# A linear-attention and two-layer MLP kernel: the first two chunks loaded in 128-row transfers, narrowed in single operations and re-ordered

## The chip, the cores and the metric

One core of a Trainium2 chip runs one program of five engines: TensorE (PE in the rows; its weight loads are PEld), VectorE (DVE), ScalarE (ACT), GpSimd (POOL) and SyncE (SP), which here only issues transfers (DMAs). The metric is the device time of one execution in microseconds, lower is better; the kernel before is given as the median of three runs.

## The reference, cut to what matters

```python
kv  = einsum('bhsd,bhse->bhde', k, v)        # 8 batches, 8 heads, 576 tokens, 64 dims
out = einsum('bhsd,bhde->bhse', q, kv)
x   = out / sqrt(mean(out * out, -1) + 1e-6) * g_norm   # -> 4608 tokens x 512
h   = x @ w_in;   y = maximum(0.01 * h, h) @ w_out      # 512 -> 2048 -> 512
h   = y @ w_in2                                          # again 512 -> 2048 -> 512
out = (P3(h) / (1 + |b0||h| + |b1|h*h + 1e-6)) @ w_out2
```

## The kernel before, in words

The 4608 tokens are worked in nine chunks of 512. All products of the two MLPs are done in three matmuls each: a value is split into a high part of reduced precision (xh, gh, w) and the rest (xl, gl), and low times high, high times high and high times low are added up (`mm3`). So one block of 128 of the 2048 hidden columns costs a chunk 12 matmuls of 128x512 for `ph` (the first product) and 12 for `y` (the second). The weights arrive as 64-bit words, 512 KB for a part (one block's first or second weight), and each part is narrowed to 32 bits on the chip before it can be used: one step on ACT (`narrow_abs`), four on DVE in a chain (`narrow`: clamp L160, shift L161, sign L164, low bits L167), then the split: `hi` on ACT (L361) and the difference `lo` (L132).

The first MLP's weights are narrowed while the first chunks already run. That start is written out by hand: the table `STARTUP` is a list of steps, and each engine gets its instructions in the order of that list, in one queue that is never re-ordered. A step is a name with arguments: `kv,b,i,at` loads tile i of the keys and values of batch b (token rows by 512 k columns and 512 v columns), `q,c,g,at` half g of the queries of chunk c, `w,k,i` weight part i of pair k; `km` adds a kv tile's products into a batch's 64x64 states (on TensorE), `ev` copies these out of PSUM (ACT); `po` multiplies the queries with the states, `sq`, `pm`, `nr`, `nw`, `bc` are the RMS norm (squares on ACT, their means on TensorE, the inverse root on ACT and DVE, its spread over the rows on TensorE), `oc` copies po out with the gain, `xw` scales it on DVE, `xh` and `xl` split it; `h`, `lk`, `gl`, `y` are the first MLP; `ab`, `na`, `hi`, `lo` narrow and split a weight part. `wu,n` issues n matmuls on a constant tile (`warm`), whose results nobody reads. A step with `,g` at its end runs its difference on POOL. Chunk 0 and the first six blocks come first, then chunk 1 with the same six blocks; the loop over `units` takes over after that, and there `prep` does the attention of the next chunk in slots between the blocks.

Transfers: SP issues them in the list's order, and with eight semaphores a ninth transfer is issued only when the one eight before it has landed. A batch has 576 tokens, so its five kv tiles have 128, 128, 128, 128 and 64 rows; a half of the queries comes as two transfers of 64 rows of the chip's memory each (`load_q`), so that the two heads of a pair lie above each other as `mm_out` wants them.

The change touches `STARTUP`, `KT`, `load_gain`, `narrow`, `load_q`, `mm_kv`, `evac_kv`, the `p_` functions of these steps, the slot of one load in `prep` and the last output copy (L724 to L731).

Of the kernel before, what the change touches and what calls it, by code (L numbers as in the profile page):

```python
# [8 lines left out]
F32 = mybir.dt.float32  # L9
F32R = mybir.dt.float32r  # L10
U32 = mybir.dt.uint32
# [11 lines left out]
    q,0,0,w0_8 q,0,1,w0_9 tl c kv,0,4,w0_10 w,0,0 kv,0,3,w0_11 kv,0,1,w0_12 kv,0,2,w1_6 kv,0,0,w1_7 wu,14 w,2,0  # L23
    w,0,1 w,1,0 kv,1,2,w1_8 kv,1,4,w0_7 wu,4 g kv,1,1,w1_9 kv,1,0,w1_5 km,0,4 kv,1,3,w0_6 wu,2 wu,6 km,0,3
    km,0,1 w,2,1 ab,0,0 na,0,0 q,1,1,raw q,1,0,raw hi,0,0 w,1,1 km,0,0 km,0,2 wu,6 ev,0 ab,0,1 po,0,1 na,0,1
    po,0,0 ab,1,0 sq,0,1 w,3,0 km,1,2 w,3,1 sq,0,3 ab,2,0 na,1,0 sq,0,2 hi,0,1 wu,8 lo,0,1,g pm,0,1 sq,0,0
    km,1,4 cg pm,0,0 w,4,0 na,2,0 lo,0,0 km,1,1 oc,0,3,w0_11 hi,1,0 oc,0,1,w0_10 nr,0,w0_8 nw,0 wu,2 lo,1,0,g
    hi,2,0 km,1,3 oc,0,0,w0_10 km,1,0 w,5,0 oc,0,2,w0_11 bc,0,0 ev,1 lo,2,0 bc,0,1 xw,0,0 xw,0,2 ab,2,1 xw,0,1
    xh,0,0 xh,0,1 po,1,1 xw,0,3 xl,0,1,g xh,0,2 xh,0,3 sq,1,3 sq,1,2 po,1,0 pm,1,1 xl,0,0 ab,1,1 sq,1,0 xl,0,3
    xl,0,2,g h,0,0 h,0,2 na,2,1 ab,3,0 oc,1,1,w0_12 ab,3,1 sq,1,1 na,1,1 w,5,1 lk,0,0 hi,2,1 na,3,1 w,4,1 w,6,1  # L30
    lo,2,1,g hi,1,1 hi,3,1 lo,1,1,g oc,1,2,w1_6 pm,1,0 oc,1,0,w0_12 nr,1,w0_9 lo,3,1 h,0,1 ab,4,1 ab,5,0
    oc,1,3,w1_6 gl,0,0 y,0,0 ab,5,1 ab,4,0 na,3,0 lk,0,1 nw,1 na,5,1 lk,0,2 hi,3,0 bc,1,1 h,0,3 gl,0,1 hi,5,1
    xw,1,3 y,0,1 xh,1,3 w,6,0 xw,1,2 lo,3,0,g na,4,1 lo,5,1,g ab,6,1 w,8,1 bc,1,0 h,0,4 lk,0,3 gl,0,2,g hi,4,1
    xh,1,2 ab,6,0 na,5,0 lo,4,1,g hi,5,0 w,8,0 na,4,0 lk,0,4 gl,0,3,g hi,4,0 xw,1,0 gl,0,4 w,7,1 lo,4,0,g
# [8 lines left out]
def kernel(  # L43
# [27 lines left out]
    KT = [(i * P, min(P, S - i * P)) for i in range((S + P - 1) // P)]  # L71
# [46 lines left out]
    def load_gain():  # L118
        for j in range(P // D):
            nc.sync.dma_start(out=gsc[j * D:(j + 1) * D, :], in_=g_norm.rearrange("(p o) -> p o", o=1))  # L120
# [35 lines left out]

    def narrow(ts, u):

        uf = u.bitcast(F32)
        nc.vector.tensor_scalar(out=uf, in0=uf, scalar1=TOP_MIN, scalar2=TOP_MAX, op0=ALU.max, op1=ALU.min)  # L160
        nc.vector.tensor_scalar(out=u, in0=u, scalar1=3, scalar2=0x3FFFFFFF,  # L161
                                op0=ALU.logical_shift_left, op1=ALU.bitwise_and)
        for i, t in enumerate(ts):
            nc.vector.scalar_tensor_tensor(out=u[:, i, :], in0=words(t, U32)[1], scalar=0xC0000000, in1=u[:, i, :],  # L164
                                           op0=ALU.bitwise_and, op1=ALU.bitwise_or)
        for i, t in enumerate(ts):
            nc.vector.scalar_tensor_tensor(out=u[:, i, :], in0=words(t, U32)[0], scalar=29, in1=u[:, i, :],  # L167
                                           op0=ALU.logical_shift_right, op1=ALU.bitwise_or)
# [73 lines left out]
    with tc.manual_schedule():  # L242
        Y = {}
        G = {}
        with ExitStack() as actx:
# [5 lines left out]
            KV = {}  # L251

            def home(at):

                if at == "raw":
                    return raw()
                return wp.tile([P, 2, N], F32, tag=at, name="raw")
# [97 lines left out]

            def w1_hi(k, i=None):
# [29 lines left out]
            nk = len(KT)  # L386
            HALF = 6
# [21 lines left out]
            def p_kv(bt, i, at="raw"):  # L409
                ss["kv", bt, i] = load_kv(bt, i, at)  # L410

            def p_km(bt, i):
                if bt not in acc:
                    acc[bt], made[bt] = bank("att" if bt else "h", "kvacc"), 0
                mm_kv(i, ss.pop(("kv", bt, i)), acc[bt], made[bt] == 0, made[bt] == nk - 1)
                made[bt] += 1

            def p_ev(bt):
                evac_kv(bt, acc.pop(bt))

            def p_q(c, g, at="raw"):
                qs[c, g] = load_q(c, g, at, (nc.sync, nc.sync if c else nc.scalar))

            def p_po(c, g):
                for p in (2 * g, 2 * g + 1):
                    po[c, p] = bank(f"y{p}", "po")
                mm_out(c, g, qs.pop((c, g)), (po[c, 2 * g], po[c, 2 * g + 1]))
# [20 lines left out]
            def p_pm(c, g):  # L448
# [3 lines left out]
                for p in (2 * g, 2 * g + 1):  # L452
                    mm_ms(p, ss.pop((c, p)), pm[c])

            def p_nr(c, at):
                t = home(at)
                rr[c], ww[c] = t[:, 0, :], t[:, 1, :]
                norm_act(pm[c], rr[c], ww[c])

            def p_nw(c):  # L460
                norm_dve(pm[c], rr[c], ww[c])

            def p_bc(c, g):
                for p in (2 * g, 2 * g + 1):
                    bc[c, p] = bank("h" if c == 0 and g == 0 else "att", "bc")
                    r = slice(32 * p, 32 * (p + 1))
                    nc.tensor.matmul(out=bc[c, p], lhsT=spread[r], rhs=ww[c][r], start=True, stop=True)
# [16 lines left out]
            def p_lk(c, f):  # L484
                if (c, f // 2) not in G:
                    G[c, f // 2] = new_g()
                t = tt[c, f] = leaky(hh.pop((c, f)))
                nc.scalar.activation(out=G[c, f // 2][0][:, f % 2, :], in_=t, func=AF.Copy)
# [12 lines left out]
            def p_table():  # L501
# [11 lines left out]
            def prep(c, po_at, ms_at, w_at, x_at, bursts):  # L513
# [46 lines left out]
                def load_w():  # L560

                    t = st["b"] = squares()
                    for j in range(P // D):
                        (nc.sync, nc.scalar)[j].dma_start(out=t[j * D:(j + 1) * D], in_=rs[c].rearrange("(p r) n -> r p n", r=32)[j:j + 1]
                                          .to_broadcast([D, NC, N]))
# [8 lines left out]
                for g in range(NC // 2):  # L574
                    at(po_at[g], "load", ldq, g)
# [136 lines left out]
        def emit_y2():  # L712
# [11 lines left out]
            else:  # L724
                for e in range(NC):
                    t = raw(1)[:, 0, :]
                    if e % 2:
                        nc.vector.tensor_copy(out=t, in_=ys[e])
                    else:
                        nc.scalar.copy(out=t, in_=ys[e])  # L730
                    nc.sync.dma_start(out=out[pc - NCH, e], in_=t)  # L731
# [83 lines left out]
```

## Time and profile before

| | us |
|---|---|
| median of 3 runs (1663.96 to 1664.95) | 1664.94 |
| the profiled execution, its own time | 1663.81 |
| its span, first to last instruction | 1661.9 |
| PE busy in the span | 1646.3 |
| DVE busy | 920.2 |
| ACT busy | 817.3 |
| POOL busy | 193.1 |

The profiled execution takes 1.9 us outside its span. PE is busy for 99% of the span, so its time is mostly a fixed amount of matmul work; the sum of busy times is an average over stages, though, and the stage that the change edits is a few per cent of the span at its start. The trace tells for each instruction when it ran, how long its engine had been idle before it, and which event ended that idle time; for the transfers, what rate a stretch had; and for TensorE the clock that was granted (1.00 is 2.4 GHz, 0.50 is 1.2 GHz).

### The profile page before, as it was taken

The page shows a single profiled execution, that of the slowest core. Times are in us where ns is not written, and L with a number is a line of the kernel's source. Part 1 is how long each engine was busy: PE and PEld are TensorE (multiplying, and loading weights), DVE is VectorE, ACT ScalarE, POOL GpSimd, SP SyncE. Part 2 cuts the span into 40 slices and gives each one's busy share as a digit, 9 for nine tenths or more (in the row PEclk, how much of TensorE's full clock was granted, in tenths as well). Part 3 has the DMA queues.
Part 4 walks back from the last instruction along what each step waited for, and adds up shares of the span by engine and source line. Part 5 has one row for each costly group of instructions (what it writes and reads, how often), then busy time and mean ns, then how long its engine had stood idle before and what let it go on. Part 6 is the DMA issues. An engine that isn't in the chain of part 4 may idle for free.

```text
span 1661.9 us, 19228 instructions
## 1 busy us (share of the span) xinstructions
PE 1646.3 (99%) x7938; PEld 1336.5 (80%) x7938; DVE 920.2 (55%) x1045; ACT 817.3 (49%) x1080; POOL 193.1 (12%) x91
## 2 busy tenths in 40 slices
PE   8999999999999999999999999999999999999999
PEld 5688778878787887878888888888888888888887
DVE  5858133333342323322337767777767677777776
ACT  4545333333433233332437566655666656666555
POOL 1300000000000000000001222122222222221221
PEclk9999999999999999999999999999999999999999
DMA  9334635152432433220421010101010100001000
GB/s 295 98 126 153 179 107 152 56 166 70 151 103 102 114 89 108 68 79 0 153 89 51 1 51 1 51 1 51 1 51 1 50 2 23 29 1 51 1 26 26
DMA packets 43175, 121.56 MB, mean 73 GB/s; under 512 B 4817, under 2 KB 4817, under 8 KB 43089
## 3 DMA queue, kind: packets, MB, share of 16 engines
q1 hardware_dynamic: 40896, 116.15, 22.1%
q10 hardware_dynamic: 2192, 4.19, 1.1%
q8 instruction: 62, 1.02, 0.3%
q14 instruction: 25, 0.20, 0.0%
HBM read 89.13 MB, written 31.20 MB: 72 GB/s over the span
## 4 chain that ended last, share of the span: by engine, by line
PE 95%; DMA 2%; DVE 2%; ACT 0%; SPq 0%; issue 0%; POOL 0%
PE ph L179 16%; PE y L181 15%; PE y L179 15%; PE y L180 15%; PE ph L181 15%; PE ph L180 15%; DMA raw<-in_kv_dram 1%; PE kvacc L280 1%; DMA raw<-in_qT_dram 1%; PE po L297 1%; DVE tmp L164 1%; PE pm L446 0%; DVE tmp L161 0%; DVE tmp L167 0%; DVE tmp L160 0%
## 5 line engine op out<-in xcount | busy, mean ns | idle before, releaser
L179 PE MATMUL ph<-xh,w 128*128 128x512 f32 x1152 | 452.1, 392 | 1.2 <-POOL w L132 1.2
L179 PE MATMUL y<-gh,w 128*128 128x512 f32 x1152 | 448.4, 389 | 1.8 <-issue 1.2
L181 PE MATMUL ph<-xl,w 128*128 128x512 f32 x1152 | 448.5, 389 | 0.0
L180 PE MATMUL ph<-xh,w 128*128 128x512 f32 x1152 | 448.4, 389 | 0.0
L181 PE MATMUL y<-gl,w 128*128 128x512 f32 x1152 | 448.2, 389 | 0.0
L180 PE MATMUL y<-gh,w 128*128 128x512 f32 x1152 | 448.1, 389 | 0.0
L132 DVE TENSOR_TENSOR gl<-t,gh 128x512 fp32r<-128x512 f32 x139 | 96.1, 691 | 432.8 <-ACT gh L642 414.2
L132 POOL TENSOR_TENSOR gl<-p,gh 128x1024 fp32r<-128x1024 f32 x70 | 169.0, 2415 | 1366.9 <-ACT gh L136 1366.9
L398 ACT ACTIVATE t<-ph 128x512 f32<-128x512 f32 x144 | 85.9, 597 | 361.8 <-PE ph L181 361.8
L179 PEld LDWEIGHTS ph<-xh,w 128*128 128x128 f32 x1152 | 216.1, 188 | 56.9 <-issue 8.8
L179 PEld LDWEIGHTS y<-gh,w 128*128 128x128 f32 x1152 | 216.3, 188 | 47.2 <-issue 1.6
L181 PEld LDWEIGHTS y<-gl,w 128*128 128x128 f32 x1152 | 216.3, 188 | 45.3 <-DVE gl L132 0.2
L181 PEld LDWEIGHTS ph<-xl,w 128*128 128x128 f32 x1152 | 216.1, 188 | 45.6 <-POOL xl L132 0.3
L180 PEld LDWEIGHTS y<-gh,w 128*128 128x128 f32 x1152 | 216.0, 188 | 44.8
L180 PEld LDWEIGHTS ph<-xh,w 128*128 128x128 f32 x1152 | 216.5, 188 | 44.0
L693 ACT ACTIVATE e<-ph,bb 128x1024 f32<-128x1024 f32 (+1 forms) x73 | 80.6, 1105 | 291.1 <-PE ph L181 291.1
L696 DVE SCALAR_TENSOR_TENSOR e<-s,b,e 128x1024 f32<-128x1024 f32 (+1 forms) x73 | 92.7, 1270 | 176.0 <-ACT s L694 176.0
L704 DVE SCALAR_TENSOR_TENSOR e<-e,z 128x1024 f32<-128x1024 f32 (+1 forms) x73 | 105.4, 1444 | 30.6 <-ACT z L701 30.5
L703 DVE SCALAR_TENSOR_TENSOR p<-p,na,ph 128x1024 f32<-128x1024 f32 (+1 forms) x73 | 92.5, 1267 | 2.6
L705 DVE SCALAR_TENSOR_TENSOR p<-p,na,z 128x1024 f32<-128x1024 f32 (+1 forms) x73 | 91.9, 1258 | 0.0
L706 DVE SCALAR_TENSOR_TENSOR p<-e,p 128x1024 f32<-128x1024 f32 (+1 forms) x73 | 88.4, 1210 | 2.5
L702 DVE TENSOR_TENSOR p<-p,ph 128x1024 f32<-128x1024 f32 (+1 forms) x73 | 87.6, 1200 | 0.0
(84 smaller groups left out, 1137.1 us busy)
## 6 DMA issues: line engine op xcount, KB each, us to landing
tmp<-in_w_dram SPq DMA_DIRECT2D x32, 512.0 KB, 6.8
raw<-in_kv_dram SPq DMA_DIRECT2D x32, 512.0 KB, 5.4
raw<-in_w_dram SPq DMA_DIRECT2D x32, 512.0 KB, 5.4
x<-raw SPq DMA_DIRECT2D x18, 512.0 KB, 3.3
raw<-x SPq DMA_DIRECT2D x18, 512.0 KB, 5.7
raw<-in_qT_dram SPq DMA_DIRECT2D x34, 256.0 KB, 5.1
w<-cv SPq DMA_DIRECT2D x16, 512.0 KB, 2.9
raw<-w SPq DMA_DIRECT2D x32, 256.0 KB, 3.0
```

The lines of the kernel that those rows point to most:

```text
L132: (nc.gpsimd if pool else nc.vector).tensor_tensor(out=lo, in0=src, in1=hi.bitcast(F32), op=ALU.subtract)
L179: nc.tensor.matmul(out=dst, lhsT=wl, rhs=xh, start=first, stop=False, **kw)
L180: nc.tensor.matmul(out=dst, lhsT=wh, rhs=xh, start=False, stop=False, **kw)
L181: nc.tensor.matmul(out=dst, lhsT=wh, rhs=xl, start=False, stop=last, **kw)
L398: nc.scalar.activation(out=t, in_=ps, func=AF.Prelu, alpha=0.01)
L693: nc.scalar.activation(out=e, in_=ph, func=AF.Abs, scale=bb[:, 0:1])
L696: nc.vector.scalar_tensor_tensor(out=e, in0=s, scalar=b1[:, 0:1], in1=e, op0=ALU.mult, op1=ALU.add)
L702: nc.vector.tensor_tensor(out=p, in0=p, in1=ph, op=ALU.mult)
L703: nc.vector.scalar_tensor_tensor(out=p, in0=p, scalar=na[:, 1:2], in1=ph, op0=ALU.add, op1=ALU.mult)
L704: nc.vector.scalar_tensor_tensor(out=e, in0=e, scalar=Q_C, in1=z, op0=ALU.add, op1=ALU.mult)
L705: nc.vector.scalar_tensor_tensor(out=p, in0=p, scalar=na[:, 0:1], in1=z, op0=ALU.add, op1=ALU.mult)
L706: nc.vector.scalar_tensor_tensor(out=p, in0=e, scalar=-2.0, in1=p, op0=ALU.add, op1=ALU.mult)
```

## The change

Nine kv tiles of 128 rows cover the first 1152 tokens in place of ten: the fifth holds the last 64 tokens of batch 0 and the first 64 of batch 1, and each batch uses its half. A half of the queries of chunks 0 and 1 is one transfer of 128 rows, heads in memory order; kv states and `po` of these chunks are laid out to match (head 2k in the upper 64 rows, head 2k+1 in the lower, matmuls on the diagonal quarters of the array), and `p_ks` afterwards re-lays batch 1's states for chunk 2. The narrowing is listed as four single steps `n1` to `n4` (and the norm as `nr ns nw nx`, and `gh` apart from `lk`), so that steps of different parts stand between each other. No step of the start runs on POOL. The warm matmuls go from 44 to 14. The gain is loaded on ACT's queue. The whole list has a new order. Outside the start, the first query half of chunk 2 is loaded two slots earlier into another tile, and the very last output copy is done in two halves on DVE and ACT, stored over two queues.

```diff
 STARTUP = """
-    q,0,0,w0_8 q,0,1,w0_9 tl c kv,0,4,w0_10 w,0,0 kv,0,3,w0_11 kv,0,1,w0_12 kv,0,2,w1_6 kv,0,0,w1_7 wu,14 w,2,0
...
+    g tl c wu,14 kv,0,0,w0_10 kv,0,3,w0_11 kv,0,4,w0_12 km,0,0 kv,0,1,w1_6 kv,0,2,w1_7 km,0,3 q,0,1,w0_7 km,0,4
...
+            nc.scalar.dma_start(out=gsc[j * D:(j + 1) * D], in_=g_norm.rearrange("(p o) -> p o", o=1))
...
+    def narrow_step(step, ts, u):
+        if step == 1:
...
     def narrow(ts, u):
...
+        for step in range(1, 5):
+            narrow_step(step, ts, u)
...
+                t = home("cv" if (c, g) == (2, 0) else "raw")
...
+                        h = 4 * (k // 2) + 2 * s + k % 2 if pair else 2 * k + s
...
+            def mm_pair(c, p, q, dst):
...
+                    for s in range(2):
+                        r = slice(s * D, (s + 1) * D)
+                        nc.tensor.matmul(out=dst[r, o], lhsT=KVP[bt][r, p, :], rhs=q[r, p % 2, o], start=True, stop=True)
...
+            def p_kv(bt, i, at):
+
+                t = ss["kv", bt, i] = home(at)
+                t0 = i * P + bt * (nk - 1) * P
+                nc.sync.dma_start(out=t, in_=kv[t0:t0 + P])
...
+                if i == (nk - 1 if bt == 0 else 0):
+                    t = ss["kv", 0, nk - 1][D * bt:D * (bt + 1)]
...
+            def p_ks():
+
+                KV[1] = kvp.tile([P, NC, D], F32, tag="kv", name="kv")
+                to, at = (t.rearrange("p (g j) e -> p j g e", j=2) for t in (KV[1], KVP[1]))
+                for s in range(2):
+                    for j in range(2):
+                        nc.vector.tensor_copy(out=to[s * D:(s + 1) * D, j], in_=at[j * D:(j + 1) * D, s])
...
+                nc.sync.dma_start(out=t, in_=qT[4 * g * D:4 * (g + 1) * D, c * N:(c + 1) * N].rearrange("(j p) n -> p j n", p=P))
...
-                    at(po_at[g], "load", ldq, g)
+                    at(0 if (c, g) == (2, 0) else po_at[g], "load", ldq, g)
...
+                    halves = [slice(0, N)] if e < NC - 1 else [slice(0, N // 2), slice(N // 2, N)]
...
+                        (nc.sync, nc.scalar)[i].dma_start(out=out[pc - NCH, e][:, o], in_=t[:, o])
```

TensorE's queue at the start, before, from the middle of batch 0's kv tiles to the spread norm, a little ahead of the first `ph` (kvacc: kv states, po: queries by states, pm: means, bc: spread norm):

```order
L280 MATMUL kvacc<-raw 64x64 x32
L406 MATMUL warm<-ones 128x512 x6
L297 MATMUL po<-raw,kv 64x512 x8
L280 MATMUL kvacc<-raw 64x64 x8
L406 MATMUL warm<-ones 128x512 x8
L446 MATMUL pm<-sq,pick 32x512 x2
L280 MATMUL kvacc<-raw 64x64 x8
L446 MATMUL pm<-sq,pick 32x512 x2
L280 MATMUL kvacc<-raw 64x64 x8
L406 MATMUL warm<-ones 128x512 x2
L280 MATMUL kvacc<-raw 64x64 x16
L467 MATMUL bc<-raw,spread 128x512 x4
```

and in the change, from the first matmul to the same place:

```order
L440 MATMUL warm<-ones 128x512 x14
L291 MATMUL kvacc<-raw 64x64 x40
L321 MATMUL po<-raw,kv 64x512 x8
L495 MATMUL pm<-sq,pick 32x512 x4
L291 MATMUL kvacc<-raw 64x64 x40
L514 MATMUL bc<-raw,spread 128x512 x4
```

The four blocks of warm matmuls between the others are gone, batch 0 is finished before anything else, and all of batch 1's tiles now stand ahead of `bc`.

DVE around the first `ph`, before (w: `lo` of a weight part, raw<-raw,bc: `xw`, xl: the low part of x, L160 to L167: the narrowing):

```order
L132 TENSOR_TENSOR w_3_386<-tmp,w_3_386 128x512
L470 TENSOR_TENSOR raw<-raw,bc 128x512 x4
L132 TENSOR_TENSOR xl_427<-raw,xh_423 128x512
L132 TENSOR_TENSOR xl_430<-raw,xh_426 128x512
L160 TENSOR_SCALAR tmp<-tmp 128x512
L161 TENSOR_SCALAR tmp<-tmp 128x512
L164 SCALAR_TENSOR_TENSOR tmp<-tmp 128x512
L167 SCALAR_TENSOR_TENSOR tmp<-tmp 128x512
```

and in the change:

```order
L517 TENSOR_TENSOR raw<-raw,bc 128x512 x3
L136 TENSOR_TENSOR w_0_352<-tmp,w_0_352 128x512
L517 TENSOR_TENSOR raw<-raw,bc 128x512
L136 TENSOR_TENSOR xl_361<-raw,xh_357 128x512
L164 TENSOR_SCALAR tmp<-tmp 128x512
L136 TENSOR_TENSOR xl_359<-raw,xh_355 128x512
L164 TENSOR_SCALAR tmp<-tmp 128x512
L136 TENSOR_TENSOR xl_360<-raw,xh_356 128x512
L136 TENSOR_TENSOR xl_362<-raw,xh_358 128x512
L166 TENSOR_SCALAR tmp<-tmp 128x512 x2
```

All four `xl` are on DVE now (two were on POOL), and single narrowing steps stand between them.

## Rows read from the trace of the kernel before

**Rows 1.** Stretches: length, then busy us of PE, PEld, DVE, ACT, POOL, clock, DMA share, GB/s.
```profile
0.00:37.40 37.40, 29.48 (x270) 18.19 (x270) 20.35 (x49) 17.21 (x31) 5.80 (x8) 0.95 0.97 311
37.40:84.00 46.60, 43.64 (x185) 32.18 (x184) 40.28 (x57) 27.42 (x49) 15.71 (x12) 1.00 0.32 102
84.00:1655.00 1571.00, 1570.51 (x7476) 1284.20 (x7475) 858.23 (x939) 771.48 (x1001) 171.63 (x72) 1.00 0.21 66
```
**Rows 2.** The chain that ended last, 0 to 140 us: start, length, what.
```profile
3.70 8.29 DMA raw<-in_kv_dram
12.01 11.58 DMA raw<-in_kv_dram
23.61 8.83 DMA raw<-in_qT_dram
...
70.25 0.23 PE ph L181
```
**Rows 3.** TensorE's timeline, 0 to 84 us: start, length, what, [idle before].
```profile
15.87 1.88 PE L280 MATMUL kvacc<-raw 128*64 128x64 f32 x32 [1.86 <-DMA raw<-in_kv_dram]
...
20.05 1.95 PE L297 MATMUL po<-raw,kv 64*64 64x512 f32 x16
...
27.57 0.69 PE L280 MATMUL kvacc<-raw 128*64 128x64 f32 x16
...
30.64 1.51 PE L467 MATMUL bc<-raw,spread 32*128 32x512 f32 x8 [0.63 <-DVE raw L307]
...
36.44 1.05 PE L446 MATMUL pm<-sq,pick 128*32 128x512 f32 x4 [0.60 <-ACT sq L436]
37.42 0.50 PE L179 MATMUL ph<-xh,w 128*128 128x512 f32 x1
...
69.52 0.50 PE L179 MATMUL ph<-xh,w 128*128 128x512 f32 x1 [1.19 <-POOL w L132]
```
**Rows 4.** Stretches of transfers and of the clock; columns as in rows 1.
```profile
2.40:8.40 6.00, 5.42 (x17) 3.96 (x15) 0.78 (x8) 1.01 (x1) 0.00 (x0) 1.00 1.04 232
...
20.00:22.00 2.00, 2.00 (x17) 0.51 (x16) 1.90 (x5) 0.38 (x1) 0.00 (x0) 1.00 1.08 256
27.00:31.00 4.00, 3.37 (x57) 2.19 (x56) 3.79 (x5) 3.28 (x7) 0.75 (x1) 1.00 1.08 221
12.60:16.00 3.40, 1.27 (x36) 0.99 (x34) 1.14 (x2) 0.63 (x1) 0.00 (x0) 1.00 1.03 410
16.00:19.40 3.40, 3.40 (x36) 3.00 (x36) 0.27 (x1) 1.05 (x2) 0.00 (x0) 0.50 1.03 410
```
**Rows 5.** Transfers issued from 39.9 to 41 us: size, us from issue to landing.
```profile
tmp<-in_w_dram SPq DMA_DIRECT2D x1, 512.0 KB, 3.5
```
**Rows 6.** DVE's timeline, 0 to 90 us; columns as in rows 3.
```profile
19.13 0.43 DVE L160 TENSOR_SCALAR tmp<-tmp 128x512 f32<-128x512 f32 x1 [5.36 <-ACT tmp L155]
19.59 0.43 DVE L161 TENSOR_SCALAR tmp<-tmp 128x512 uint32<-128x512 uint32 x1
...
24.95 1.66 DVE L164 SCALAR_TENSOR_TENSOR tmp<-tmp 128x512 uint32<-128x512 uint32 x1
...
31.83 2.48 DVE L470 TENSOR_TENSOR raw<-raw,bc 128x512 f32<-128x512 f32 x4 [0.74 <-PE bc L467]
...
47.07 0.69 DVE L132 TENSOR_TENSOR w<-tmp,w 128x512 fp32r<-128x512 f32 x1 [0.70 <-ACT w L361]
...
79.09 1.37 DVE L132 TENSOR_TENSOR w<-tmp,w 128x512 fp32r<-128x512 f32 x1 [1.22 <-ACT w L361]
```
**Rows 7.** POOL's timeline, 20 to 90 us; columns as in rows 3.
```profile
24.79 1.27 POOL L132 TENSOR_TENSOR w<-tmp,w 128x512 fp32r<-128x512 f32 x1 [24.35 <-ACT w L361]
```
**Rows 8.** TensorE's timeline at 180 us.
```profile
180.28 0.77 PE L297 MATMUL po<-raw,kv 64*64 64x128 f32 x10 [0.49 <-DMA raw<-in_qT_dram]
```
**Rows 9.** DVE's timeline at the end: its last copy.
```profile
1657.75 0.69 DVE L728 COPY raw<-y 128x512 f32<-128x512 f32 x1 [0.67 <-PE y L181]
```

More of the change, by code (lines that the diff above doesn't have):

```diff
@@ L155, in narrow_abs @@
             nc.scalar.activation(out=u[:, i, :].bitcast(F32), in_=words(t, F32)[1], func=AF.Abs)
-    def narrow(ts, u):
[L159 to L168, printed above, removed]
+    def narrow_step(step, ts, u):
+        if step == 1:
+            uf = u.bitcast(F32)
+            nc.vector.tensor_scalar(out=uf, in0=uf, scalar1=TOP_MIN, scalar2=TOP_MAX, op0=ALU.max, op1=ALU.min)
+        elif step == 2:
+            nc.vector.tensor_scalar(out=u, in0=u, scalar1=3, scalar2=0x3FFFFFFF,
+                                    op0=ALU.logical_shift_left, op1=ALU.bitwise_and)
+        elif step == 3:
+            for i, t in enumerate(ts):
+                nc.vector.scalar_tensor_tensor(out=u[:, i, :], in0=words(t, U32)[1], scalar=0xC0000000, in1=u[:, i, :],
+                                               op0=ALU.bitwise_and, op1=ALU.bitwise_or)
+        else:
+            for i, t in enumerate(ts):
+                nc.vector.scalar_tensor_tensor(out=u[:, i, :], in0=words(t, U32)[0], scalar=29, in1=u[:, i, :],
+                                               op0=ALU.logical_shift_right, op1=ALU.bitwise_or)
+    def narrow(ts, u):
+        for step in range(1, 5):
+            narrow_step(step, ts, u)
     def new_w(f, part):
@@ L354, in w1_narrow, with w1_part_narrow, fn @@
                     narrow(x[:2][sl], x[2][:, sl, :])
+            def w1_part_narrow(step):
+                def fn(k, i):
+                    x, sl = w1_half(k, i)
+                    narrow_step(step, x[:2][sl], x[2][:, sl, :])
+                return fn
             def w1_hi(k, i=None):
@@ L386 @@
             nk = len(KT)
+            assert S % P == D and nk * P == S + D
             HALF = 6
@@ L446, in mm_ms, with p_pm, p_norm, step @@
                 nc.tensor.matmul(out=dst[32 * p:32 * (p + 1)], lhsT=pick, rhs=x, start=True, stop=True)
-            def p_pm(c, g):
+            def p_pm(c, p):
                 if c not in pm:
                     pm[c] = bank("att", "pm")
[L452 to L467, printed above, removed]
+                mm_ms(p, ss.pop((c, p)), pm[c])
+            def p_norm(fn):
+                def step(c, at=None):
+                    if at:
+                        t = home(at)
+                        rr[c], ww[c] = t[:, 0, :], t[:, 1, :]
+                    fn(pm[c], rr[c], ww[c])
+                return step
+            def p_bc(c, p):
+                bc[c, p] = bank("h" if c == 0 and p < 2 else "att", "bc")
+                r = slice(32 * p, 32 * (p + 1))
+                nc.tensor.matmul(out=bc[c, p], lhsT=spread[r], rhs=ww[c][r], start=True, stop=True)
             def p_xw(c, p):
@@ L726, in emit_y2 @@
                     t = raw(1)[:, 0, :]
[L727 to L731, printed above, removed]
+                    halves = [slice(0, N)] if e < NC - 1 else [slice(0, N // 2), slice(N // 2, N)]
+                    for i, o in enumerate(halves):
+                        if (e + i) % 2:
+                            nc.vector.tensor_copy(out=t[:, o], in_=ys[e][:, o])
+                        else:
+                            nc.scalar.copy(out=t[:, o], in_=ys[e][:, o])
+                    for i, o in enumerate(halves):
+                        (nc.sync, nc.scalar)[i].dma_start(out=out[pc - NCH, e][:, o], in_=t[:, o])
         for c in range(NCH):
```

112 lines of the change are left out of this document (61 added, 51 removed).

## The prediction

> **What bounds the kernel now.** First the busy time by stretch. From 84 to 1655 us TensorE is busy for 1570.51 of 1571.00 us [rows 1]: nothing in the start can shorten that matmul work, it can only begin earlier. From 0 to 37.40 us it is busy too, but with preparation and with warm matmuls whose results nobody reads; from 37.40 to 84.00 us it works at the first MLP and misses 46.60 - 43.64 = 2.96 us [rows 1]. So the time is the moment of the first `ph` (37.42 us [rows 3]), plus the gaps after it, plus fixed work.
>
> Then the chain of waits, for what sets 37.42: three transfer pieces (8.29, 11.58 and 8.83 us) fill almost all of it up to 32.44 us [rows 2]. The transfer stretches say why: at 2.4, 20 and 27 us the engines are busy all the time (share over 1.0) at 232, 256 and 221 GB/s, while a stretch of 128-row transfers has 410 [rows 4]. These three slow stretches are the 64-row ones: the first queries, a 64-row kv tile, the second queries.
>
> Then DVE's timeline for the gaps after 37.40: it is busy for 40.28 of 46.60 us there [rows 1], a low-bits or sign step of 0.69 us takes 1.66 us when POOL works beside it [rows 6, 7], and the longest TensorE gap (1.19 us at 69.52) is ended by a POOL difference [rows 3].
>
> **The change, part by part.**
>
> A. *The first `ph`.* Ahead of it now stand nine kv tiles of 512 KB, two query halves and two weight parts: 13 transfers, all of 128 rows. A first one lands 3.5 us after its issue [rows 5], issued at about 0.7: 4.2 us. The others follow at 524 KB / 410 GB/s = 1.28 us: the last kv tile lands at 4.2 + 12 x 1.28 = 19.6. Its products take 0.69 [rows 3], so `bc` starts at 20.3; from `bc` to the first `xw` it was 31.83 - 30.64 = 1.19 us [rows 3, 6], so DVE starts `xw` at 21.5. Until the last `xl` it has nine differences or products and two clamps. One of the first costs 0.61 (2.48 us for four, the last of 0.69 [rows 6]); that is an overlap of 0.08, and 0.43 - 0.08 = 0.35 is my estimate for a clamp that waits for no result of its neighbour. 9 x 0.61 + 2 x 0.35 = 6.2, so the last `xl` is ready at 27.7. Nine of that block's twelve matmuls can be done before it, at 0.23 each [rows 2], so `ph` starts in effect at 27.7 - 2.0 = 25.7. **37.4 - 25.7 = 11.7 us less.** The other way to `bc` is the norm of chunk 0: the last queries land at 4.2 + 6 x 1.28 = 11.9, half a `po` is 0.98 [rows 3], and before it took 8.6 us from the end of `po` (22.0) to `bc` (30.64) with batch 1's tiles in between [rows 3]: 21.5 at worst, 1.2 us later than 20.3. I take 20.3, since in the new order no tile stands between `po` and the means; 1.2 is the bad end.
>
> B. *The means of chunk 1.* Half of them stood before the first `ph` (1.05 us [rows 3]), all stand behind it now: **+1.0**.
>
> C. *The gaps after it.* Before: 2.96 us. In the change, from the first `ph` to the low part of chunk 0's sixth block, DVE has 22 clamps and shifts and 47 longer operations, by the list: 22 x 0.35 + 47 x 0.61 = 36.4 us. TensorE has 13 blocks of 12 matmuls, the means (2.1) and `bc` (1.5): 13 x 12 x 0.23 + 3.6 = 39.5. So DVE has 3.1 us in hand, though it starts with two parts ready where before there were four. With POOL's share taken over it does more operations, but none is stretched: a POOL difference of 1.27 us cost DVE 1.66 - 0.69 = 0.97 [rows 6, 7] and costs 0.61 on DVE itself. Single steps in turn save the wait for one's own result (0.46 from clamp to shift [rows 6] against 0.35). Bounds: no gap at all, or all 46.60 - 40.28 = 6.3 us of DVE's idle time stays, less 3.1: 3.2 us. I take 1.5, in the middle: **-1.5**.
>
> D. *The warm matmuls.* Removing 30 of them saves nothing, as TensorE waits there for transfers. They may have held the clock. From 12.6 to 16.0 TensorE was busy for 1.27 of 3.40 us, in short kv products, and in the stretch behind it the granted clock was 0.50, that is 1.2 GHz; it came back to 2.4 GHz while warm matmuls and kv products filled the stretch [rows 4]. In the change the kv products stand alone in two places, so the clock will fall at least once. At 1.2 GHz two kv tiles took 1.88 us [rows 3], `po`, means and `bc` would double. Best end 0 (it falls only where TensorE waits anyway), worst end 4.9 (the rival below). I take **+1.0**, nearer to the good end, because most of the work up to 20 us waits for transfers. The Trainium skill (TensorE: Matmul & The Clock Gate, "HAM oscillation") lets the clock fall when TensorE idles for a while between bursts. By it D would be 0 and the sum 1651.9, since the gaps here are shorter than the ones it warns of; the row at 16.0 disagrees, since the longest gap before it was 1.86 us.
>
> E. *Chunk 2's queries.* The 0.49 us gap at 180 us [rows 8] waits for a transfer that is issued two slots earlier now: **-0.5**. If its new tile came free too late the gap would stay: 0.
>
> F. *The end.* The last copy of 0.69 us [rows 9] is halved and its transfer shared by two queues: **-0.35**; at worst 0.
>
> The four copies of `p_ks`, the gain on ACT's queue and the split `gh` cost nothing: DVE and ACT are at about half load after the start [rows 1], and the gain is needed only after `po`. Without that cover they are under 2 us together.
>
> **Sum:** -11.7 + 1.0 - 1.5 + 1.0 - 0.5 - 0.35 = -12.05. Made against the profiled execution (1663.81) this is 1651.8; that one lies 1.1 us under the median shown, and I take the difference off the median: 1664.94 - 12.05 = **1652.9**.
>
> **The rivals.**
>
> *The clock stays at 1.2 GHz up to `ph`.* For: rows 4 and the removal of the warm matmuls. `po` and means of chunk 0 (2.0 and 2.1 us [rows 3]) then take 4 us more, of which I take half as hidden, since batch 1's tiles land meanwhile; `bc` costs 1.2 more, and 3.4 us of `ph` at half speed, as long as the slow stretch of rows 4, cost 1.7: 4.9 in place of 1.0, so 1656.8. Against: `po` and the means are dense by themselves. Beside it, the Trainium skill (the same page, "The HAM clock gate") calls the slow clock the default that only activity lifts.
>
> *The queries stay slow.* Their rows are still 2 KB long. If that and not the 64 rows made 221 GB/s, a half takes 2.4 us, two halves 2.3 us more ahead of `bc`, and everything later lands later too: 2.3 to 4.6, taken 3.4: 1656.3. Against: the kv tile at 20 us has rows of 4 KB and is as slow, at 256 [rows 4].
>
> *The single steps wait for ACT, and it gets slower.* On DVE, from 28 us on, some 30 operations need a result of ACT just made (10 clamps, 10 `lo`, 6 `gl`, 4 `xl`), and DVE's queue cannot pass a waiting one; before, a chain of four steps gave ACT time. Such waits were 0.70 and 1.22 us [rows 6]. With w each, TensorE loses 30 w - 3.1; without gaps the time is 1651.4. From w = 0.67 on it is slower than before by over 0.2%; 0.70 gives 1669.3, 1.22 gives 1685. For: DVE has only 3.1 us in hand. Against: before, 6.3 us of idle in the whole stretch [rows 1], over 57 operations.
>
> *It does not do what it says:* transfers of 128 rows at 410 GB/s were there before, so this is only the query case.
>
> **How the numbers follow.** 0.2% (3.3 us) is about what a measurement can tell from no change. Forecast 0.70; slow clock 0.12; slow queries 0.05; waits for ACT 0.13, of which 0.05 end between 1655 and 1661, 0.04 within 0.2% (w near 0.5 to 0.67) and 0.04 slower. So faster 0.92, same 0.04, slower 0.04. Range: with C and D at their good ends 1650.4, and 1 us more if the first transfer lands early: 1649.0. With A's 1.2, C's 1.7 and D's 3.9 more, their bad ends, it would be 1659.7; I stop at 1659.5, which leaves out most of the waits for ACT.
>
> **What would show it.** Right: kv and query transfers at about 410 GB/s from 4 us on; the first `ph` at 24 to 27 us; DVE without idle time from 25 to 60 and no operation stretched; TensorE without gaps over 0.5 us after 28. Wrong: a granted clock of 0.50 over the first `ph` (clock), query stretches near 220 GB/s (queries), many DVE waits for ACT of 0.5 us and more and TensorE gaps ended by `w` or `gl` (waits).

## The result, and the profile after

| | before | after |
|---|---|---|
| median of four runs each on one chip, us | 1664.95 | 1650.65 |
| range of the runs, us | 1663.96 to 1664.99 | 1650.42 to 1650.84 |
| the profiled execution, its own time | 1663.81 | 1650.42 |
| its span | 1661.9 | 1648.6 |

The ratio is 0.9915, interval 0.9898 to 0.9933. So the change is faster by 0.85%, that is 14.3 us by the medians and 13.3 us by the spans; 1652.9 had been forecast, from 1649.0 to 1659.5.

The busy line of the page after. TensorE has lost 1646.3 - 1639.8 = 6.5 us of work (the stretches of warm matmuls alone went from 13.84 to 5.60 us, while `po` of chunk 0 took 3.31 more), and the span 13.3: half of the time that went was not work of TensorE.

```profile
PE 1639.8 (99%) x7910; PEld 1331.6 (81%) x7910; DVE 915.2 (56%) x1066; ACT 817.2 (50%) x1081; POOL 169.3 (10%) x74
```

Stretches after, with the columns of [rows 1]: the start up to the first `bc`, from there to 70 us, and the rest.

```profile
0.00:24.50 24.50, 19.65 (x205) 11.85 (x206) 7.80 (x33) 9.75 (x17) 0.20 (x4) 0.93 0.90 335
24.50:70.00 45.50, 45.28 (x214) 32.07 (x211) 42.70 (x81) 31.37 (x57) 0.00 (x0) 1.00 0.48 167
70.00:1640.00 1570.00, 1570.00 (x7477) 1283.96 (x7476) 862.91 (x950) 774.49 (x1006) 169.10 (x70) 1.00 0.21 67
```

The second row answers to the second of [rows 1]: TensorE misses 45.50 - 45.28 = 0.22 us where it missed 2.96, POOL does nothing, DVE is busy for 94%. The third misses nothing.

TensorE's timeline after, columns as in [rows 3].

```profile
12.95 5.26 PE L321 MATMUL po<-raw,kv 64*64 64x512 f32 x16 [0.74 <-DMA raw<-in_qT_dram]
18.14 2.00 PE L495 MATMUL pm<-sq,pick 128*32 128x512 f32 x8
...
23.06 0.69 PE L291 MATMUL kvacc<-raw 128*64 128x64 f32 x16 [0.63 <-DMA raw<-in_kv_dram]
23.68 1.66 PE L514 MATMUL bc<-raw,spread 32*128 32x512 f32 x8
25.27 3.69 PE L321 MATMUL po<-raw,kv 64*64 64x64 f32 x32
28.89 0.50 PE L190 MATMUL ph<-xh,w 128*128 128x512 f32 x1
...
35.00 1.06 PE L495 MATMUL pm<-sq,pick 128*32 128x512 f32 x8
36.28 0.47 PE L190 MATMUL ph<-xh,w 128*128 128x512 f32 x1 [0.22 <-DVE w L136]
```

The order of the reading: the last kv tile lands at 23.02 (23.06 is its product), `bc` follows its products at once, and the first `ph` stands at 28.89 where it stood at 37.42. What is new is `po` of chunk 0: 5.26 us in place of 1.95 [rows 3].

DVE's timeline after, same columns: the first three `xw`, the last two of the four `xl`, and the only wait over 0.5 us between 24.5 and 70.

```profile
24.83 1.88 DVE L517 TENSOR_TENSOR raw<-raw,bc 128x512 f32<-128x512 f32 x3
...
29.71 1.28 DVE L136 TENSOR_TENSOR xl<-raw,xh 128x512 fp32r<-128x512 f32 x2
...
54.10 0.69 DVE L136 TENSOR_TENSOR w<-tmp,w 128x512 fp32r<-128x512 f32 x1 [0.71 <-ACT w L394]
```

From the first `xw` to the end of the last `xl` it is 30.99 - 24.83 = 6.16 us. No operation is stretched as in [rows 6].

Transfers and the clock after; columns as in [rows 1].

```profile
4.70:8.90 4.20, 3.38 (x40) 2.50 (x38) 0.15 (x1) 0.00 (x0) 0.00 (x0) 1.00 0.81 304
8.90:12.80 3.90, 2.05 (x48) 1.64 (x48) 0.00 (x0) 0.37 (x1) 0.00 (x0) 1.00 1.03 404
12.82:16.22 3.40, 3.27 (x8) 1.10 (x10) 0.00 (x0) 0.60 (x1) 0.00 (x0) 0.50 1.04 390
```

From 8.9 us on the rate is the 400 GB/s of a 128-row stretch, for kv tiles and queries. From 4.70 to 8.90 it is 304 with the engines busy for only 0.81. The 13 transfers land at 4.71, 6.87, 8.90, 10.16, 11.49 (kv), 12.82, 14.17 (queries), 15.43, 16.70 (weights), 18.08, 20.42, 21.70 and 23.02 (kv), by the semaphores that the trace shows them raise. Nine of the twelve steps are 1.26 to 1.38 us; three are 2.16, 2.03 and 2.34.

**Where the 13.3 us came from**, span against span: 8.53 from the earlier first `ph`, then 3.29 up to the start of the 401st matmul of `ph` and `y` (136.08 before, 124.26 after), of which 2.96 - 0.22 = 2.74 are gaps; 1.0 from there to the last matmul, with the gap of [rows 8] gone; 0.41 behind the last matmul (4.14 before, 3.73 after). Sum 13.23.

### The profile page after: what moved, and what is told of

Same layout as the page of the kernel before. It is cut to its first block, busy times and chain, and to the rows that moved or that the text cites. A ratio compares the mean times of both kernels' runs of the same rounds, so it can differ in the third digit from the quotient of the medians.

```text
span 1648.6 us, 19154 instructions
## 1 busy us (share of the span) xinstructions
PE 1639.8 (99%) x7910; PEld 1331.6 (81%) x7910; DVE 915.2 (56%) x1066; ACT 817.2 (50%) x1081; POOL 169.3 (10%) x74
## 4 chain that ended last, share of the span: by engine, by line
PE 98%; DVE 1%; DMA 1%; issue 0%; SPq 0%; ACT 0%
PE ph L190 16%; PE y L190 16%; PE y L191 16%; PE y L192 16%; PE ph L191 16%; PE ph L192 16%; PE kvacc L291 1%; PE po L308 1%; DMA raw<-in_qT_dram 1%; PE pm L495 0%; PE po L321 0%; DVE tmp L170 0%; SPq L447 0%; DVE tmp L166 0%; DVE tmp L164 0%
## 5 line engine op out<-in xcount | busy, mean ns | idle before, releaser
L136 DVE TENSOR_TENSOR gl<-t,gh 128x512 fp32r<-128x512 f32 x144 | 99.4, 691 | 426.9 <-ACT gh L693 413.5
```

The costliest lines, as they stand in the source:

```text
L136: (nc.gpsimd if pool else nc.vector).tensor_tensor(out=lo, in0=src, in1=hi.bitcast(F32), op=ALU.subtract)
```

## The experiments

All are compared by their ratio to the kernel before, run beside them on the same chip; the change itself has 0.9915, and 0.001 is 1.7 us. My theory: the gain comes from the earlier first `ph` (transfers of 128 rows, order) and from the gaps (single steps, no POOL), the warm matmuls and the edits at the end are worth little. The rivals: that one of the parts does it alone, or that the part is not needed.

### What delays the first transfers, and what the clock costs

Two of the three slow steps lie beside the gain's two transfers on ACT's queue, 64 rows of 4 bytes each, which landed at 5.59 and 8.09. So the gain was moved behind them (first diff), warm matmuls were put back between the first kv products (second), and both.

```diff
-    g tl c wu,14 kv,0,0,w0_10 ...
-    km,0,1 q,0,0,w1_5 km,0,2 ev,0 w,0,1 ...
+    tl c wu,14 kv,0,0,w0_10 ...
+    km,0,1 q,0,0,w1_5 km,0,2 ev,0 g w,0,1 ...
```

> The change with one edit: the two gain transfers (64 rows of 4 bytes each) are issued on ACT after the states of batch 0 have been copied out, not first. In the change the second and third kv tile landed 2.16 and 2.03 us after the one before them, all others 1.27 to 1.38. Theory: the gain's 4-byte pieces hold up the kv tiles; now all land 1.28 apart, batch 0 is complete 1.6 us earlier, the first ph starts up to 1.6 us earlier than 28.9, time 1649.0 to 1650.0. Rival: the start of the queue itself is slow; spacing and time stay as they are (1650.6).

```diff
-    ... km,0,3 q,0,1,w0_7 km,0,4
-    km,0,1 q,0,0,w1_5 km,0,2 ev,0 ...
+    ... km,0,3 wu,2 q,0,1,w0_7 km,0,4 wu,2
+    km,0,1 wu,2 q,0,0,w1_5 km,0,2 wu,2 ev,0 ...
```

> The change with two warm matmuls behind each of four kv tiles of batch 0 (8 in all, about 0.5 us each time, in gaps of 0.6 to 0.9 us). Theory: the clock fell to 0.50 at 12.8 us because of the short kv products before it; with the warm matmuls it stays at 1.00, po of chunk 0 takes 3.5 in place of 5.3 us, and bc can start when the last kv tile has landed, which it waited for anyway: ph 0 to 0.5 us earlier, time 1650.1 to 1650.7. Rival: the norm was the later one, ph 1.7 earlier, 1649.0.

> Both edits. Theory: the late gain moves the transfers 1.6 us earlier, and with the clock up the norm follows: ph at 27.3, time 1649.0 (1648.5 to 1649.5), less than the late gain alone by up to 0.5. Rival: one of the two is hidden behind DVE's work, and it ends where the better of them does.

The gain late: 1651.6 us, ratio 0.9928 [0.9916, 0.9941]. Batch 0's last tile landed at 10.07 in place of 11.49. The steps of 2.16 and 2.03 us became 1.28 and 1.75, so the gain's pieces do delay their neighbours, by 1.2 us together; the other 0.2 is an earlier first landing, and one long step is left without them. But nothing came of it. TensorE's timeline and one stretch of this run, then DVE and ACT:

```profile
23.56 2.33 PE L514 MATMUL bc<-raw,spread 32*128 32x512 f32 x8 [0.98 <-DVE raw L334]
...
30.71 0.50 PE L190 MATMUL ph<-xh,w 128*128 128x512 f32 x1
```

```profile
25.10:28.40 3.30, 3.30 (x15) 1.18 (x16) 3.30 (x7) 2.13 (x5) 0.00 (x0) 0.50 0.95 323
```

```profile
19.14 0.15 DVE L127 TENSOR_SCALAR gsc<-gsc 128x1 f32<-128x1 f32 x1 [15.67 <-DMA gsc<-in_g_norm_dram]
...
19.33 0.69 ACT L492 ACTIVATE raw<-po,gsc 128x512 f32<-128x512 f32 x1 [1.70 <-DVE gsc L127]
```

The last kv tile still landed at 21.85, 1.17 us earlier than in the change. But `bc` waited 0.98 us for the norm of chunk 0 (L334), which had been ready in time before, and the clock fell a second time, over the end of `bc` and over `po` of chunk 1. The norm was late because the gain was: moved, it landed at 19.12 in place of 8.09. DVE's scaling of it (L127) waited for that, with every narrowing step behind it in the queue, and so did ACT's first copy of `po` with the gain (L492), with the norm's own steps behind that. The theory named the delay rightly and the price wrongly: it expected the whole delay back and had no term for the gain's own use.

The warm matmuls back: 1650.24, 0.9917 [0.9904, 0.9931]. Two stretches and `po`:

```profile
8.70:12.60 3.90, 3.90 (x59) 2.59 (x55) 0.00 (x0) 0.00 (x0) 0.00 (x0) 1.00 1.03 406
12.80:16.20 3.40, 3.40 (x16) 1.07 (x17) 0.00 (x0) 1.58 (x4) 0.00 (x0) 1.00 1.03 384
```

```profile
13.21 3.65 PE L321 MATMUL po<-raw,kv 64*64 64x512 f32 x16
...
22.68 0.69 PE L291 MATMUL kvacc<-raw 128*64 128x64 f32 x16 [0.62 <-DMA raw<-in_kv_dram]
23.30 1.66 PE L514 MATMUL bc<-raw,spread 32*128 32x512 f32 x8
```

The clock stays at 1.00, that is 2.4 GHz, over `po`, which takes 3.65 us in place of 5.26; the first `ph` came at 28.51, 0.38 earlier. All of the 0.38 is already there at the last kv tile (22.64 in place of 23.02), and `bc` follows that tile's products at once in both runs. The time is equal within the interval. So D's cost is at most 0.4 us by the medians and nothing by the trace: the fall is there and lies beside transfers. Both edits together: 1650.81, 0.9926 [0.9913, 0.9938], first `ph` 28.45, `bc` again 0.71 behind L334, and the gain again late, at 18.49. So these two runs show what the pieces cost the tiles, but not what the start would be worth without that delay: a place for the gain in between, where it comes in time for its own use, was not tried.

### No POOL, and single steps

The seventeen differences that ran on POOL before the change were put back there:

```diff
-    ... hi,0,1 n4,0,0 w,1,1 lo,0,1 bc,0,1 xw,0,1
+    ... hi,0,1 n4,0,0 w,1,1 lo,0,1,g bc,0,1 xw,0,1
...
-    xh,0,1 w,3,0 xl,0,2 ... xl,0,1 xl,0,3
+    xh,0,1 w,3,0 xl,0,2,g ... xl,0,1,g xl,0,3
```

> The change with the 17 differences that ran on POOL before sent to POOL again (same order otherwise). Theory: each stretches a DVE step by about 0.97 us and saves 0.61 on DVE; 17 x 0.36 = 6.1 us more against DVE's 2.8 us of idle time from 24.5 to 70: 2 to 5 us slower, 1652.7 to 1655.7, with TensorE gaps ended by POOL. Rival: the order hides it, no change (1650.6).

1654.24, 0.9942 [0.9929, 0.9956], first `ph` 28.61. DVE's and TensorE's timelines:

```profile
43.55 1.52 DVE L166 TENSOR_SCALAR tmp<-tmp 128x512 uint32<-128x512 uint32 x1
```

```profile
43.13 0.50 PE L190 MATMUL y<-gh,w 128*128 128x512 f32 x1 [0.84 <-POOL w L136]
```

A stretched operation is back (a shift is 0.43 us alone [rows 6]; this one lies beside two POOL differences that run from 40.60 to 44.79 us), and so are TensorE's gaps ended by POOL. That is the theory's side: 3.6 us slower than the change by the medians, 4.5 by the ratios (whose intervals just touch).

Then the four narrowing steps of a part were listed together again, once where the first stood and once where the last stood:

```diff
-    ab,0,1 sq,0,1 pm,0,2 kv,1,3,w1_9 n1,0,1 pm,0,0 ...
+    ab,0,1 sq,0,1 pm,0,2 kv,1,3,w1_9 n1,0,1 n2,0,1 n3,0,1 n4,0,1 pm,0,0 ...
```

> The change with the four narrowing steps of each weight part listed together where the first of them stood; nothing else moves. Theory: a chain waits for its own results, 0.46 for 0.35 us once and 0.73 for 0.61 twice, 0.35 us a part, 12 parts behind the first ph: 4.2 us against 2.8 us of DVE idle, and some steps come early ahead of more urgent ones: 1 to 4 us slower, 1651.6 to 1654.6. Rival: single steps matter little, 1650.6.

```diff
-    nr,0,w1_5 km,1,0 n2,0,1 km,1,3 q,1,1,raw km,1,2 ns,0 n3,0,1 n1,0,0 oc,0,3,w0_11 n4,0,1 oc,0,0,w0_10
+    nr,0,w1_5 km,1,0 km,1,3 q,1,1,raw km,1,2 ns,0 oc,0,3,w0_11 n1,0,1 n2,0,1 n3,0,1 n4,0,1 oc,0,0,w0_10
```

> The change with the four narrowing steps of a part listed together where the last of them stood (in the earlier run they stood where the first one did, 11.3 us slower). DVE's operations ahead of every split, xl and gl are then the same set as in the change. Theory (what cost 11.3 us was steps of later parts ahead of urgent ones): only the waits for own results remain, 0.35 us a part, 12 parts, 4.2 us against some 2 us of idle time: 1 to 3 us slower than the change. Rival (single steps are worth what was lost, wherever the chain stands): about 11 us slower again.

Together at the first's place: 1661.9, 0.9985 [0.9976, 0.9994]; the first `ph` stood at 29.43, but then:

```profile
32.46 0.50 PE L192 MATMUL ph<-xl,w 128*128 128x512 f32 x1 [2.30 <-DVE xl L136]
...
35.31 0.80 PE L192 MATMUL ph<-xl,w 128*128 128x512 f32 x1 [1.89 <-DVE xl L136]
```

```profile
33.50:40.20 6.70, 4.89 (x12) 3.83 (x13) 6.46 (x12) 3.31 (x7) 0.00 (x0) 0.50 0.46 158
```

DVE is busy, but with steps that nobody needs yet, while `xl` stands behind them; TensorE waits, and its clock falls over the first blocks. One of the eleven executions kept a mean clock of 0.999, where the others had 0.994 to 0.997, and took 1659.01: by that one, some 2.9 us of the loss go with the clock. Together at the last's place: 1657.75, 0.9961 [0.9947, 0.9975], first `ph` 28.70. DVE, then TensorE:

```profile
34.47 0.69 DVE L136 TENSOR_TENSOR w<-tmp,w 128x512 fp32r<-128x512 f32 x1 [1.71 <-ACT w L394]
```

```profile
40.35 0.50 PE L190 MATMUL ph<-xh,w 128*128 128x512 f32 x1 [1.77 <-DVE w L136]
```

Now the steps come late: the part's `hi` on ACT can start only behind the whole chain, and `lo`, the next on DVE, waits 1.71 us for it. Both expectations were too small (1 to 4 and 1 to 3 us; 11.3 and 7.1 by the medians). Spreading the steps is worth far more than the 0.11 us a step that a wait for one's own result costs: it lets urgent operations through on the one side and gives ACT time for `hi` on the other.

### The rows of a transfer

The four query transfers were split into two of 64 rows each, everything else as in the change; then the kv tiles too.

```diff
-                nc.sync.dma_start(out=t, in_=qT[...].rearrange("(j p) n -> p j n", p=P))
+                src = qT[...].rearrange("(j p) n -> p j n", p=P)
+                for s in range(2):
+                    nc.sync.dma_start(out=t[s * D:(s + 1) * D], in_=src[s * D:(s + 1) * D])
```

> The change with each of the four query transfers of the start split into two of 64 rows (same tile, same layout). Theory: 64 rows halve the rate: 2.4 in place of 1.3 us for a query half, 2.3 us more ahead of the last kv tile and 4.6 ahead of the last queries; ph 2.3 to 4.6 us later, 1653 to 1655.5. Rival: rows of 2 KB or the two queues were the cause before; then the rate stays near 400 GB/s and the time at 1650.6.

```diff
-                nc.sync.dma_start(out=t, in_=kv[t0:t0 + P])
+                for s in range(2):
+                    nc.sync.dma_start(out=t[s * D:(s + 1) * D], in_=kv[t0 + s * D:t0 + (s + 1) * D])
```

> The same with the nine kv tiles split into two transfers of 64 rows as well. Theory: 13 transfers of 512 KB (nine kv, four query) take 1.15 us more each, 15 us in all by the last queries, 12.6 by the last kv tile; ph 12 to 15 us later at about 42, and the weight parts behind them later too: 1661 to 1666, which takes back all or nearly all of the change. Rival: the new order carries the gain: under 1656.

Queries only: 1656.93, 0.9956 [0.9944, 0.9968]. Stretches with the queries of chunk 0 and of chunk 1, and the first `ph`:

```profile
12.00:16.00 4.00, 3.47 (x23) 1.69 (x25) 0.00 (x0) 0.37 (x1) 0.00 (x0) 0.59 1.06 255
24.50:27.00 2.50, 0.67 (x16) 0.53 (x16) 2.46 (x4) 1.43 (x3) 0.00 (x0) 1.00 1.08 224
```

```profile
33.64 0.50 PE L190 MATMUL ph<-xh,w 128*128 128x512 f32 x1
```

Tiles and queries: 1663.16, 0.9995 [0.9987, 1.0004], which takes back the whole change, as expected.

```profile
5.00:18.00 13.00, 7.44 (x90) 5.42 (x90) 0.15 (x1) 0.37 (x1) 0.00 (x0) 0.82 1.04 232
25.00:31.00 6.00, 2.46 (x41) 2.33 (x43) 4.13 (x8) 3.00 (x6) 0.00 (x0) 0.66 1.04 230
```

```profile
41.97 0.50 PE L190 MATMUL ph<-xh,w 128*128 128x512 f32 x1
```

The same bytes, in the same lengths of row, run at 224 to 255 GB/s in 64-row transfers and at 390 to 404 in 128-row ones. The number of rows does it, not the 2 KB of a query row. One rival is left: the split also halves a transfer's size, and no run loads 256 KB over 128 rows. Two readings speak against it. The DMA engines count as busy for all of the slow stretches (shares of 1.04 to 1.08), so there is no pause between the halves; and a store of 256 KB from 128 rows, alone from 718.19 to 719.02 us in the change, ran at 313 GB/s with its start and end counted in.

### The edits at the far end

Chunk 2's first query half back in its slot and tile, the last output in one copy:

```diff
-                t = home("cv" if (c, g) == (2, 0) else "raw")
+                t = home("raw")
...
-                    at(0 if (c, g) == (2, 0) else po_at[g], "load", ldq, g)
+                    at(po_at[g], "load", ldq, g)
...
-                    halves = [slice(0, N)] if e < NC - 1 else [slice(0, N // 2), slice(N // 2, N)]
+                    halves = [slice(0, N)]
```

> The change with its two small parts undone: chunk 2's first queries loaded at their old slot and place, the last output copied and stored in one piece. Theory: the 0.49 us gap at chunk 2's po comes back and the end is 0.35 us longer: 1651.5. Rival: nothing of either is left, 1650.6.

1650.51, 0.9918 [0.9904, 0.9931]: nothing. Its TensorE at chunk 2's `po` and DVE's last copy, beside those of the change:

```profile
174.13 1.09 PE L308 MATMUL po<-raw,kv 64*64 64x128 f32 x16
...
1644.89 0.69 DVE L781 COPY raw<-y 128x512 f32<-128x512 f32 x1 [0.67 <-PE y L192]
```

```profile
174.18 1.09 PE L308 MATMUL po<-raw,kv 64*64 64x128 f32 x16
...
1644.94 0.42 DVE L781 COPY raw<-y 128x256 f32<-128x256 f32 x1 [0.67 <-PE y L192]
```

No gap before `po` in either, so the gap of [rows 8] did not go by the earlier load; it went with something else, most likely the changed timing of the start. The shorter copy is there (0.42 in place of 0.69), yet from the last matmul to the end it is 3.73 us with it and 3.64 without.

### One part alone, on the list of before

The kernel before without POOL (every `,g` taken out), and the code of the change with the list of before: old order, chains, POOL, 44 warm matmuls, but 128-row transfers and the new layouts.

```diff
-    po,0,0 ab,1,0 ... sq,0,2 hi,0,1 wu,8 lo,0,1,g pm,0,1 sq,0,0
+    po,0,0 ab,1,0 ... sq,0,2 hi,0,1 wu,8 lo,0,1 pm,0,1 sq,0,0
```

> The kernel before with its 17 POOL differences put on DVE, old order and old transfers. Theory (POOL's neighbourhood stretches DVE steps): each costs 0.61 on DVE in place of 0.97 of stretching, and TensorE's gaps that POOL ended (1.19 us) go: 1 to 3 us faster than the kernel before. Rival (the old order counted on POOL): DVE becomes the bound in that order and it is no faster or slower.

```diff
-    g tl c wu,14 kv,0,0,w0_10 kv,0,3,w0_11 kv,0,4,w0_12 km,0,0 kv,0,1,w1_6 kv,0,2,w1_7 km,0,3 q,0,1,w0_7 km,0,4
+    q,0,0,w0_8 q,0,1,w0_9 tl c kv,0,4,w0_10 w,0,0 kv,0,3,w0_11 kv,0,1,w0_12 kv,0,2,w1_6 kv,0,0,w1_7 wu,14 w,2,0
...
```

> The code of the change with the list of the kernel before (its order, chains of four, POOL differences and warm matmuls), and only the 128-row transfers and the layouts that go with them new. Theory (transfers bring the first ph forward in any order): up to the last chunk-1 queries the old order loads 5 weight parts, 9 kv tiles and 4 query halves, 18 x 1.28 + 4.2 = 26 against 34.7 us before: ph 6 to 9 us earlier than 37.4, and the time 1656 to 1661, if DVE keeps up. Rival (the new order is what turns early data into an early ph): DVE, POOL and the slower quarter layout of po hold the old order at 1662 to 1665.

Without POOL alone: 1660.41, 0.9979 [0.9970, 0.9988], 3.5 us faster where 1 to 3 had been expected. The first `ph` even came later (38.50 for 37.42), but behind it TensorE missed 0.39 us instead of 2.96:

```profile
37.40:84.00 46.60, 46.21 (x201) 34.56 (x198) 39.80 (x70) 29.21 (x51) 0.00 (x0) 1.00 0.37 124
```

Transfers and layouts alone: 1663.27, 0.9996 [0.9987, 1.0005], nothing, though chunk 1's last queries landed at 29.0 where they had landed at 34.7. The rival's range was right. The chain of waits of this run in two pieces, and TensorE's timeline:

```profile
21.20 0.69 PE kvacc L287 x16
21.89 2.04 PE warm L436 x8
23.92 0.98 PE pm L491 x4
24.90 1.23 PE kvacc L287 x32
26.13 1.01 PE pm L491 x4
```

```profile
30.11 1.51 PE L510 MATMUL bc<-raw,spread 32*128 32x512 f32 x8 [1.10 <-DVE raw L330]
...
36.90 0.50 PE L186 MATMUL ph<-xh,w 128*128 128x512 f32 x1
```

In the old list a batch-1 tile and eight warm matmuls stand ahead of the means of chunk 0. That tile landed at 21.16, where it had landed at 22.30: of the 5.7 us that the transfers had gained by chunk 1's last queries, it had got only 1.1. So the norm still ends late and `bc` waits for it (L330). Of the rival's reasons, POOL and the slower layout of `po` do not stand in this chain. The faster transfers pay only with the new list.

### A version that might beat both

The warm matmuls as above, and the four `xl` of chunk 0 ahead of three narrowing operations, so that the first block is complete earlier:

```diff
-    ... xh,0,2 lo,0,0 xh,0,0 ...
-    xh,0,1 w,3,0 xl,0,2 n1,1,1 po,1,1 xl,0,0 ab,1,0 n1,1,0 xh,0,3 ... xl,0,1 xl,0,3
+    ... xh,0,2 xh,0,0 ...
+    xh,0,1 w,3,0 xl,0,2 po,1,1 xl,0,0 ab,1,0 xh,0,3 ... xl,0,1 xl,0,3 lo,0,0 n1,1,1 n1,1,0
```

> The change with the warm matmuls between batch 0's kv tiles (0.4 us faster in the earlier run), and the split of the second weight part and two clamps listed behind the four xl of chunk 0. Theory: the last xl is 1.3 us earlier, the first block loses its 0.5 us of stalls, but DVE's sum of work is unchanged and sets the third block: 0 to 0.5 us faster than with the warm matmuls alone, 1649.7 to 1650.3. Rival: DVE's lead is gone and later blocks wait: slower than 1650.7.

1651.44, 0.9925 [0.9912, 0.9938], first `ph` 29.37, as the last kv tile landed at 23.50 in this run (22.64 with the warm matmuls alone). TensorE's timeline:

```profile
37.46 0.47 PE L190 MATMUL ph<-xh,w 128*128 128x512 f32 x1 [1.35 <-DVE w L136]
```

The delayed weight part is 1.35 us late at the third block, as the rival had it: from the first `ph` to the 400th matmul this run takes 0.78 us longer than the one with the warm matmuls alone. By their ratios the two are equal within the intervals. No version was clearly faster than the change; the warm matmuls alone are equal to it, too.

## Why the prediction was right, point by point

The sign, the mechanism and nearly the size held: 12.05 us less was forecast, 14.3 was measured by the medians. That the sum came so close is partly luck. A was too large by 3.3 us, B, C and D erred the other way by 1.0, 1.2 and at least 0.6, and E and F gave nothing. As measured, A (8.53 by the first `ph`) and C (2.74) make 11.3 of the 13.3 us of the spans; 0.55 more lies between the first `ph` and the 401st matmul and 1.4 behind it, and no term stands for these.

*What bounds it: held.* With TensorE full from 70 us on, the whole gain lies before 140 us but for 1.4 us.

*A (-11.7): the chain held, its first link did not.* The sign given for it, a first `ph` at 24 to 27 us with 410 GB/s from 4 us on, did not come: `ph` stood at 28.89, and such a rate held from 8.9 on only. From the last kv tile's landing to `bc` it was 0.66 us (0.69 taken), from `bc` to the first `xw` 1.15 (1.19), from there to the last `xl` 6.16 (6.2). But that tile landed at 23.02, not at 19.6: of the twelve steps that were taken at 1.28 us, three were longer by 2.7 together, the first landing was 0.5 late, and the other nine steps add 0.26. So `ph` started in effect at 30.99 - 2.0 = 28.99, and A was worth 8.4. "All of 128 rows" was read for the big transfers only, and the gain had been costed at nothing for its data: two transfers of 256 bytes on another queue. That its pieces slow the first two steps is shown by moving them (1.28 and 1.75 in place of 2.16 and 2.03). That the third step, at 20.42, is due to a packet of 16 KB of the program's own instructions (1.08 us on one DMA engine, at 17.77 us) is read from traces only, and was not tried. Such a packet at 17.81 us in the run with POOL and at 18.46 in the one without the edits at the end is followed by a step of 2.17 and of 2.01; but with the warm matmuls one at 16.28 is followed by 1.29 and 1.50 only, and a step of 2.14 stands ahead of it. So this cause stays open.

*B (+1.0): 0.* The four means of chunk 1 run in one block of 1.06 us, as long as two took before [rows 3].

*C (-1.5): -2.74*, the good end of its bounds. In the new list single steps and no POOL were both needed: with POOL 0.27% is lost, with chains 0.46 to 0.70%. In the old list leaving out POOL was enough: TensorE missed 0.39 us there in spite of the chains, behind a first `ph` that came 9.6 us later than in the change.

*D (+1.0): at most 0.4, and nothing by the trace.* The granted clock did fall to 0.50, 1.2 GHz, as forecast, at 12.8 us in the stretch behind the short kv products. It cost `po` 5.26 - 3.65 = 1.6 us, which the norm had in hand, since `bc` waited for the tile at 23.02. The rule of the Trainium skill (TensorE: Matmul & The Clock Gate, "HAM oscillation"), that idle time between bursts lets the clock fall, gave 0 for D; the result is near to that, but not for its reason: the clock fell with no idle gap over 0.87 us from TensorE's first matmul up to there.

*E (-0.5) and F (-0.35): 0 each.* The gap of [rows 8] is gone without the earlier load too, and the end is no longer without the halved copy. So the 1.0 and 0.41 us that were gained behind the 401st matmul are not theirs. In the kernel before without POOL, which has neither edit, the stretch from there to the last matmul is shorter by 0.97 as well; and the end took from 3.72 to 4.02 us in the runs with the halved copy.

*A step that was left out:* `po` in the new layout takes 3.65 us at full clock for chunk 0 where 1.95 was taken over from before. The records say why: before, four matmuls started together every 0.43 us, on all four quarters of the array; on the diagonal quarters two do. It cost nothing that the trace shows: `po` of chunk 0 lies beside the transfers, and `po` of chunk 1 ends at 28.96, just as `ph` must start to be held by the last `xl`.

*The rivals.* The slow clock over `ph` did not come in the change (it did over the first blocks in the version with chains at the first step's place). The queries ran at 390 GB/s, and splitting them cost 6.3 us by the medians, more than the 3.4 that the rival had taken for slow queries: the last kv tile landed 4.07 us later (27.09 for 23.02), where 2.3 had been taken, and the first `ph` came 4.75 later. Waits of DVE for ACT were one of 0.71 us; the rival's mechanism exists, 1.71 us in one wait, but on the other side: with the steps in chains, not in turn.

## What to carry to other kernels

When a start is bound by transfers, count the rows of each one before its bytes, and count the small ones on other queues as well; a small one that is moved out of the way must still land in time for its own use. A faster transfer pays only when the queue order lets its consumer be the next thing on its engine: here the transfers alone were worth nothing, and the new list lost all its gain without them. On an in-order engine that feeds two others, spread a long chain as single steps and leave between them the time that the other engine needs.

## What was not expected of the hardware

- Two transfers of 64 rows of 4 bytes on another queue: the two 512 KB transfers beside them took 2.16 and 2.03 us from landing to landing, and 1.28 and 1.75 with the two moved away.
- 64x64 quarters used two at a time on the diagonal took 3.65 us for what four at a time did in 1.95.
- A DVE operation with one input, too, was stretched beside POOL: a shift took 1.52 us in place of 0.43.
- The granted clock fell behind a stretch of short products with 2.05 us of work in 3.90 and no idle gap over 0.87.
